# Low words of the experts' weights on one engine, matmuls over ones at the start, and later loads for one attention block, in a fused attention and mixture-of-experts kernel

## The chip, the cores and the metric

The kernel runs on one core of a Trainium2 chip. The metric is the device time of one execution in microseconds (us), as the median of several runs. TensorE (PE) does the matmuls, with its weight loads shown apart (PEld); VectorE (DVE), ScalarE (ACT) and GpSimd (POOL) do elementwise work; SyncE's queue (SPq) issues nearly all DMA transfers.

## The reference

Three stages run one after the other on 4 x 576 = 2304 tokens of 512 features.

```python
# attention: 8 heads of 64, causal window of 128, ALiBi bias, softmax
scores = scale * np.matmul(q, k.transpose(0, 1, 3, 2))
scores = np.where(mask, scores + bias[None], -1000000000.0)
attn = np.exp(scores - np.max(scores, axis=-1, keepdims=True))
x = (attn / (np.sum(attn, axis=-1, keepdims=True) + 1e-09)) @ v
...
# dense feed-forward, 512 -> 2048 -> 512
h = x @ w_in
x = (h - np.tanh(h)) @ w_out
...
# 8 experts, top 1 by cosine similarity, 512 -> 1024 -> 512
expert_idx = np.argmax(xn @ en.T / tau, axis=1)
for e in range(E):
    h = np.maximum(x[mask] @ w1[e], 0.0)
    out[mask] = gate_w[mask, None] * (h @ w2[e])
```

## The kernel before, in words

**Number format.** Most large matmuls are split: an operand becomes a high word (a rounded copy) and a low word (the rest), and three products of the words are added up. For each weight tile of an expert (128 x 512) `e_weight` issues a load into one of six staging tiles `est`, a cast on ACT (`hi`, line 1080) and a subtraction (`lo`, line 1084). The planner may put `lo` on DVE or on POOL, and it frees the staging tile.

**Attention.** The tokens are 18 blocks of 128 rows. A block is done in four quarters of two heads: `scores` (matmuls, line 485 in the first four blocks, 491 later), `soft` (adds the bias tile of the head and takes the extremum, line 513, DVE), `exp` (line 527, ACT), a transpose of the probabilities (lines 548 and 552 early, a transposing DMA at 542 later) and the product with the values (562 early, 573 later). `x_out` transposes the finished block into `xT` (lines 664, 671, 672). Blocks 0 to 3 use the keys and queries unsplit. From block 4 on they are split (`qk_half`: a load into the staging tile `stk`, an ACT cast at line 381, a subtraction at line 385), and so are the values (`v_half`: lines 443 to 454). As block 4 also looks back at block 3, `qk_half` and `v_half` run for block 3's keys and values too. There is one staging tile `stk`, and SPq issues in order: a second load into `stk` waits until line 385 has read the first, and everything behind it in the queue waits as well.

**Bias.** `consts` loads a table (`tmp`) and makes one bias tile for each head from it (line 255): heads 0 and 1 on DVE, heads 2 to 7 on POOL.

**Feed-forward.** Two blocks form a group, so there are nine groups. A `step` makes two slices of 128 hidden features: matmuls into `h` (line 712), tanh on ACT (717), a subtraction (720), high and low word (725, 729), then matmuls into `acc` (736). Eight steps finish a group. All 32 weight tiles of `w_in` and `w_out` stay in SBUF; each is loaded packed (line 335) and unpacked by lines 339, 342, 347 and 351 on ACT and DVE, in the first 80 us.

**Routing and experts.** `route` takes a group's result, finds each token's expert (line 826, the small operations of `chain` at 847 to 852, matmuls at 862 to 865) and scatters the rows. The experts (lines 1186 to 1246) follow; their weights are loaded and split while the last group of the feed-forward still runs, and then one expert ahead.

**Order.** Every operation is a task with a due time and a cost for each engine that may do it. `Plan.order` simulates the engines: it takes the task that can start earliest, then the one with the lowest due time, and picks the engine that would finish it first. The result is a fixed order of instructions for each engine; each engine runs its list in order. The due unit is one step of the feed-forward. Tasks with `port=True` are not started on DVE, in the simulation, while POOL works.

Of the kernel before, what the change touches and what calls it, by code (L numbers as in the profile page):

```python
# [13 lines left out]
BF16 = mybir.dt.bfloat16  # L14
# [3 lines left out]
AF = mybir.ActivationFunctionType  # L18
ALU = mybir.AluOpType
# [20 lines left out]
NF = 4  # L40
# [7 lines left out]
WLEAD2 = 6  # L48
N0 = 1
NPX = 16  # L50
NALT = 8
NOWN = 8
NXO = 2
# [2 lines left out]
QK = 2  # L56
# [122 lines left out]
class Builder:  # L179
# [61 lines left out]
    def zero(self, P):  # L241
        for n, t in enumerate(self.wz):
            P.add({"DVE": 0.6}, lambda e, t=t: self.nc.vector.memset(t, 0), -30, w=[("wz", n)])

    def consts(self, P):
        nc, i = self.nc, self.i
        at = {}

        def tmp(e):
            at[0] = self.at.tile([128, 512], F32, tag="xr", name="tmp", bufs=1)  # L250
            nc.sync.dma_start(out=at[0][:, 0:384], in_=i["c_bias"])

        P.add({"SP": 0.55}, tmp, -20, w=[("xr", m) for m in range(4)])
        for h in range(H):
            P.add({"DVE": 0.3} if h < 2 else {"POOL": 0.88}, lambda e, h=h: self.eng(e).tensor_scalar(
                out=self.bias[:, h, :], in0=at[0][:, 0:256], scalar1=2.0 ** -(h + 1), scalar2=None, op0=ALU.mult),
                -20 + h, r=[("xr", 0)], w=[("bias", h)])
        P.add({"POOL": 0.5}, lambda e: nc.gpsimd.tensor_copy(out=self.tri, in_=at[0][:, 256:384]), -11,
              r=[("xr", 0)], w=["tri"])
# [197 lines left out]
    def quarter(self, P, a, due):  # L457

        nc = self.nc
        b, qd = divmod(a, 4)  # L460
        hf, qq = divmod(qd, 2)
        s, n = b % 2, (2 * b + hf) % 2
        one = b in NOPRE
        W = 128 if one else 256
        v = {"sc": [None, None], "mx": [None, None]}
        pb = a % 2 if a < NPX else 0
        early = b < NF
# [3 lines left out]
        own = 1 if a < NOWN and a % 2 else None  # L471
        bank = "acc" if a < NALT and a % 2 else "sc"

# [140 lines left out]
        for jj in range(2):  # L614
            if early:
                P.add({"PE": 0.3 if one else 0.42}, lambda e, jj=jj: scores(jj), due,
                      r=["at", ("qf", b)] + [("kf", x) for x in ([b] if one else [b, b - 1])], w=[(bank, jj)])
            else:
                P.add({"PE": 0.13 if one else 0.24}, lambda e, jj=jj: scores(jj), due,
                      r=["at"] + ks + [("kl", x, hf) for x in kv] + q, w=[(bank, jj)])  # L620
        for jj in range(2):
            P.add({"DVE": ttr}, lambda e, jj=jj: soft(jj), due, r=["at", ("bias", qd * 2 + jj)],
                  w=[(bank, jj), ("mx", jj, a % 2)])
        for jj in range(2):
            P.add({"ACT": 0.49 if one else 0.64}, lambda e, jj=jj: exp(jj), due,
                  r=["at", (bank, jj), ("mx", jj, a % 2)], w=[("p32", pb, jj), ("sm", sk, qq, jj)])
        sm = [("sm", sk, x, y) for x in range(2) for y in range(2)]
        half = [("xr", 2 * hf), ("xr", 2 * hf + 1)]
        if early:
# [3 lines left out]
                  r=["at", ("tp", a)] + ([("h", own)] if own is not None else []), w=[("pt", a % 2)],  # L633
                  free="misc" if own is None else None)
            P.add({"PE": 0.45 if one else 0.9}, pv_f, due,
                  r=["at", ("pt", a % 2)] + [("vf", x) for x in ([b] if one else [b - 1, b])], w=[("o", qq)] if qq else ["o", ("o", 0), ("o", 1)])
            if qq:
# [4 lines left out]
              w=[("ph", a % 2)], port=True)  # L642
        P.add({"POOL": 0.84, "DVE": 0.46} if one else {"POOL": 1.19, "DVE": 0.71}, s_lo, due,
              r=["at", ("p32", pb, 0), ("p32", pb, 1), ("ph", a % 2)], w=[("ph", a % 2, 1)], port=True)
        P.add({"SP": 0.7 if one else 1.2}, tr, due, late=LATE, r=["at", ("ph", a % 2), ("ph", a % 2, 1)], w=[("pt", a % 2)])
        P.add({"PE": 0.28 if one else 0.56}, pv, due,
              r=["at", ("pt", a % 2)] + [("vt", x, hf, m) for x in kv for m in range(3)], w=["o"])
# [412 lines left out]
    def e_weight(self, P, e, kind, f, due):  # L1060

        nc, i = self.nc, self.i
        ff = f + FE // 128 * (e % 2)
        n = self.nld % NST
        self.nld += 1
        key, st = (kind, ff), ("est", n)
        v = {}
        w1, w2 = [i[w].rearrange("e k f -> (e k) f") for w in ("w1", "w2")]

        def load(_):  # L1070
            t = v["x"] = self.ex.tile([128, 512], F32, tag=f"est{n}", name="est")
            if kind == "i":
                half, k = divmod(f, KD)
                nc.sync.dma_start(out=t, in_=w1[bass.ds(self.at_row[e][0] + k * 128, 128), half * 512:(half + 1) * 512])
            else:
                nc.sync.dma_start(out=t, in_=w2[bass.ds(self.at_row[e][1] + f * 128, 128), :])

        def hi(_):
            t = self.w[key] = self.wp.tile([128, 2, 512], F32R, tag=f"w{kind}{ff}", name=f"e{kind}{ff}")
            nc.scalar.copy(out=t[:, 0, :], in_=v["x"])  # L1080

        def lo(eng):
            t = self.w[key]
            self.eng(eng).tensor_tensor(out=t[:, 1, :], in0=v["x"], in1=t[:, 0, :].bitcast(F32), op=ALU.subtract)

        P.add({"SP": 0.73}, load, due - 4, r=["at", ("place", e)], w=[st], lag=LAG)
        P.add({"ACT": 0.65}, hi, due, r=[st], w=[(key, 0), (key, 1)])
        P.add({"DVE": 0.72, "POOL": 1.32}, lo, due, r=[st, (key, 0)], w=[(key, 1)], port=True)

    def e_rows(self, P, v, t, due):  # L1090

# [249 lines left out]
    def build(self):  # L1341
        tc, nc = self.tc, self.nc
        for n in ("kf", "qf", "vf", "sums", "oh4", "qst", "xr", "acc", "w"):
            setattr(self, n, {})
        self.setup()
        dp = self.pool("dr", bufs=1, space=DRAM, tilewait=False)
        self.bucket = dp.tile([ROWS, ROW], F32, name="bucket")
        self.pa = dp.tile([2 * N0, 128, DM], F32, name="pa")
        self.nw = 0
        self.sent, self.puts = [], []  # L1350
        P = Plan()
        P.add({"POOL": 2.7}, lambda e: self.small(), 0, w=["small", "cum"])
        self.zero(P)
        self.consts(P)
        self.small_loads(P, -19)
        all_f = list(range(FP))
        fa, fb = all_f[:FA], all_f[FA:]
        visits = ([(g, fa) for g in range(N0)] + [(N0, all_f)] + [(g, fb) for g in range(N0)]
                  + [(g, all_f) for g in range(N0 + 1, NG)])

        def weights(fps, due, rate):
            for x, fp in enumerate(fps):
                for kind in "io":
                    for f in (2 * fp, 2 * fp + 1):
                        self.weight(P, kind, f, due + x * rate + 1.2 * (kind == "o"))

        weights(fa, -WLEAD, WRATE)
        p, xi, seen = 0, 0, set()
        for g, fps in visits:
            sl = [xi % XR, (xi + 1) % XR]  # L1370
            xi += 2
            rate = RATE if g <= N0 else 1.0
            for n in range(2):
                b = 2 * g + n
                d0 = p - 8 * rate - (LEADM if g > N0 else LEAD) + 4 * n * rate
                if g not in seen:
                    for hf in range(2):
                        due = d0 + 2 * hf * rate
                        self.qk_half(P, b, hf, due - QK)
                        if b < NF and hf == 0:  # L1380
                            self.qk_early(P, b, due - QK - 2)
                            self.v_full(P, b, due)
                        if b >= NF - 1:
                            self.v_half(P, b, hf, due)
                        for qq in range(2):
                            self.quarter(P, 4 * b + 2 * hf + qq, due + qq * rate)
                if g not in seen:
                    self.x_out(P, b, sl[n], d0 + 4 * rate)
                    if b == 0:
                        self.emb(P, 0)  # L1390
            if g == N0:
                weights(fb, p + len(fa) - WLEAD2, WRATE2)
            for fp in fps:
                self.step(P, p, g, fp, sl, fp == fps[0], fp == fps[-1])
                for e in range(E):
                    if p == PAD + e // PADN:
                        self.pad(P, e, p)
                p += 1
            if g < N0 and g not in seen:
                self.spill(P, p - 1, g, sl)  # L1400
            else:
                if g == NG - 1:
                    self.moe2(P, p, lambda: self.route(P, g, sl, p))
                else:
                    self.route(P, g, sl, p + 1)
                if g == NG - 3:
                    self.choose(P, p + 2)
                    self.space(P, p + 2)
            seen.add(g)
        with tc.manual_schedule():  # L1410
            for fn, e in P.order({"misc": 1}):
                fn(e)
        self.overflow()
        while self.open:
            k = list(self.open)[-1]
            self.close(k)
# [190 lines left out]
```

## Time and profile before

| | us |
|---|---|
| median of 3 runs (lowest to highest) | 781.98 (780.95 to 782.5) |
| profiled execution: device time | 785.27 |
| profiled execution: span of the trace | 783.4 |
| TensorE busy / its weight loads busy | 760.1 / 678.7 |
| DVE / ACT / POOL busy | 549.5 / 427.9 / 382.6 |

The span goes from the first to the last instruction of one execution, and the device time has 1.9 us more around it. Matmuls are pipelined and their ends are modelled, so a busy share near 100% on TensorE doesn't mean that it works at its peak. The granted clock is a column of the view of stretches: 1.00 stands for 2.4 GHz and 0.50 for 1.2 GHz.

### The profile page before, as it was taken

What the parts mean: (1) busy time and instruction counts of PE and PEld (TensorE: products, weight loads), DVE (VectorE), ACT (ScalarE), POOL (GpSimd) and SP (SyncE); (2) the same over time, 40 slices, a digit from 0 to 9 for tenths busy, and PEclk for the clock granted to TensorE, in tenths of its full rate; (3) what the DMA queues carried; (4) which work ended last, traced back from release to release, by engine and by line L of the source; (5) the groups of instructions that cost most, each with busy time, mean ns of one, the idle gap of its engine ahead of it and who ended that gap; (6) DMA issues with size and microseconds to landing.
All of it is one profiled execution on the core that took longest, in us unless ns stands there. A gap on an engine that the chain in (4) does not pass through costs nothing.

```text
span 783.4 us, 15248 instructions
## 1 busy us (share of the span) xinstructions
PE 760.1 (97%) x5189; PEld 678.7 (87%) x5189; DVE 549.5 (70%) x1454; ACT 427.9 (55%) x969; POOL 382.6 (49%) x378
## 2 busy tenths in 40 slices
PE   6998999999999999999999999989999999999996
PEld 4877899889998999989899998979879898888895
DVE  4888887888777688778777776887626678675420
ACT  4878776655565465555645643645235565555321
POOL 3226023674666165364744732687216577655411
PEclk9999999999999999999999999999999999999998
DMA  7996169966365353554454243764257879897100
GB/s 269 385 372 195 44 200 296 247 155 113 108 131 139 69 116 104 119 117 133 95 123 121 62 81 88 184 201 148 76 160 208 230 218 261 216 237 218 44 29 30
DMA packets 152454, 124.25 MB, mean 159 GB/s; under 512 B 115301, under 2 KB 119397, under 8 KB 152112
## 3 DMA queue, kind: packets, MB, share of 16 engines
q1 hardware_dynamic: 149344, 111.39, 53.5%
q0 software_dynamic: 3024, 11.82, 4.1%
q8 instruction: 42, 0.69, 0.4%
q14 instruction: 44, 0.36, 0.2%
HBM read 84.29 MB, written 22.06 MB: 136 GB/s over the span
## 4 chain that ended last, share of the span: by engine, by line
PE 87%; DVE 4%; issue 4%; ACT 2%; POOL 2%; DMA 1%; SPq 0%; POOLq 0%
PE h L712 25%; PE acc L736 23%; PE he L1186 12%; PE y L1221 10%; PE o L573 3%; PE sc L491 3%; PE y L1217 3%; PE of L562 2%; PE sc L485 1%; PE misc L548 1%; PE misc L664 1%; PE ht L1306 1%; DMA tmp<-in_c_bias 1%; PE misc L821 1%; DVE xA L1146 0%
## 5 line engine op out<-in xcount | busy, mean ns | idle before, releaser
L712 PE MATMUL h<-xT,wi 128*128 128x256 f32 x1728 | 227.8, 286 | 0.8 <-DVE xT L672 0.5
L712 PEld LDWEIGHTS h<-xT,wi 128*128 128x128 f32 x1728 | 219.7, 193 | 6.8 <-DVE xT L672 0.7
L736 PE MATMUL acc<-wo,gh 128*128 128x512 f32 x576 | 183.4, 400 | 0.4 <-DVE wo L351 0.4
L736 PEld LDWEIGHTS acc<-wo,gh 128*128 128x128 f32 x576 | 101.0, 190 | 16.6 <-issue 1.0
L736 PE MATMUL acc<-wo,gl 128*128 128x512 f32 x288 | 113.0, 392 | 0.0
L717 ACT ACTIVATE t<-h 128x512 f32<-128x512 f32 x72 | 43.0, 597 | 105.7 <-PE h L712 100.2
L1221 PE MATMUL y<-eo,ge 128*128 128x512 f32 x336 | 88.0, 398 | 0.2 <-ACT yo L1229 0.2
L527 ACT ACTIVATE p<-sc,mx 128x256 f32<-128x256 f32 (+1 forms) x128 | 59.0, 462 | 39.4 <-DVE mx L513 27.4
L1221 PEld LDWEIGHTS y<-eo,ge 128*128 128x128 f32 x336 | 60.1, 188 | 10.5 <-ACT yo L1229 0.4
L729 DVE TENSOR_TENSOR gl<-t,gh 128x512 fp32r<-128x512 f32 x72 | 64.4, 895 | 6.7 <-ACT gh L725 6.4
L537 POOL TENSOR_TENSOR ph<-p,ph 128x512 f16<-128x512 f32 (+1 forms) x37 | 43.9, 1187 | 51.1 <-ACT ph L532 40.5
L736 PEld LDWEIGHTS acc<-wo,gl 128*128 128x128 f32 x288 | 54.3, 189 | 12.2
L385 POOL TENSOR_TENSOR khl<-stk,khl 64x512 fp32r<-64x512 f32 x24 | 31.8, 1325 | 67.3 <-ACT khl L381 61.3
L720 DVE TENSOR_TENSOR t<-h,t 128x512 f32<-128x512 f32 x72 | 49.5, 687 | 18.5 <-ACT t L717 18.2
L1208 DVE SCALAR_TENSOR_TENSOR ge<-he,ge 128x256 fp32r<-128x256 f32 x104 | 28.8, 315 | 46.7 <-ACT ge L1202 46.3
L513 DVE CUSTOM_DVE_ANT_0 sc<-sc,bias 128x256 f32<-128x256 f32 (+1 forms) x136 | 49.6, 374 | 15.5 <-PE sc L491 9.5
L1246 POOL DMA_INDIRECT out<-yo,ix x23 | 25.0, 1089 | 69.9 <-ACT yo L1242 63.0
L1202 ACT ACTIVATE ge<-he 128x288 fp32r<-128x288 f32 (+2 forms) x56 | 23.2, 414 | 61.2 <-PE he L1186 42.5
L1186 PEld LDWEIGHTS he<-xA,ei 128*128 128x128 f32 x384 | 54.1, 189 | 2.6
L1186 PE MATMUL he<-xA,ei 128*128 128x288 f32 (+2 forms) x384 | 56.0, 296 | 0.0
L1186 PEld LDWEIGHTS he<-xT,ei 128*128 128x128 f32 x384 | 53.5, 188 | 2.2
L1186 PE MATMUL he<-xT,ei 128*128 128x288 f32 (+2 forms) x384 | 55.0, 295 | 0.0
(224 smaller groups left out, 1444.3 us busy)
## 6 DMA issues: line engine op xcount, KB each, us to landing
est<-in_w SPq DMA_DIRECT2D x128, 256.0 KB, 3.6
bucket<-in_c_pad SPq DMA_DIRECT2D x8, 1155.0 KB, 9.7
rawi<-in_w_in SPq DMA_DIRECT2D x16, 511.8 KB, 7.3
rawo<-in_w_out SPq DMA_DIRECT2D x16, 511.8 KB, 8.9
stk<-in_k SPq DMA_DIRECT2D x30, 256.0 KB, 2.8
stq<-in_q SPq DMA_DIRECT2D x28, 256.0 KB, 3.0
vst<-in_v SPq DMA_DIRECT2D x30, 128.0 KB, 2.8
xe<-bucket SPq DMA_DIRECT2D x3, 384.0 KB, 3.4
```

The lines of the kernel that those rows point to most:

```text
L385: self.eng(e).tensor_tensor(out=k, in0=r4("k")[64:128], in1=k.bitcast(F32), op=ALU.subtract)
L513: nc.vector.tensor_tensor_reduce(out=x, in0=x, in1=self.bias[:, h, c0:c1], scale=-0.125, scalar=mx[:, 1:2] if m else 3.0e38, op0=ALU.add, ...
L527: nc.scalar.activation(out=v["p32"][:, jj * W:(jj + 1) * W], in_=x, func=AF.Exp, scale=-1.0, bias=v["mx"][jj][:, 0:1], accum_out=self.sums ...
L537: self.eng(e).tensor_tensor(out=ph[:, 2 * W:4 * W], in0=v["p32"][:, 0:2 * W], in1=ph[:, 0:2 * W], op=ALU.subtract)
L712: nc.tensor.matmul(h3(v["h"], f2), lhsT=w[:, a, k, :], rhs=xT[c][:, :, k, :], start=(k == 0 and n == 0), stop=(k == KD - 1 and n == 2))
L717: nc.scalar.activation(out=v["t"], in_=v["h"].rearrange("p a b -> p (a b)"), func=AF.Tanh)
L720: nc.vector.tensor_tensor(out=v["t"], in0=v["h"].rearrange("p a b -> p (a b)"), in1=v["t"], op=ALU.subtract)
L729: self.eng(e).tensor_tensor(out=v["gl"], in0=v["t"], in1=v["gh"].bitcast(F32), op=ALU.subtract)
L736: nc.tensor.matmul(self.acc[g, t], lhsT=v[a][:, c0:c0 + 128], rhs=self.w["o", fs[f2]][:, c, :], start=(first and f2 == 0 and n == 0), stop ...
L1186: nc.tensor.matmul(h[:, 0:N], lhsT=w[:, a, c0:c0 + 128], rhs=xT()[b][:, k, 0:N], start=(k == 0 and n == 0), stop=(k == KD - 1 and n == 2))
L1208: nc.vector.scalar_tensor_tensor(out=g[:, o:o + c1 - c0], in0=hk[f][:, c0:c1], scalar=0.0, in1=g[:, c0:c1].bitcast(F32), op0=ALU.max, op1= ...
L1221: nc.tensor.matmul(y[t], lhsT=gt(f, a)[:, (t - ts[0]) * 128:(t - ts[0] + 1) * 128], rhs=self.w["o", f0 + f][:, b, :], start=(f == 0 and n ...
```

## The change

There are three edits. (1) The low words of the experts' weights are no longer offered to POOL. (2) A bf16 tile `fill` of ones is set by DVE, and 21 matmuls of 128 x 512 over it go to the PSUM bank `h0`, whose result nobody reads: 7 before everything else, 8 behind the scores of quarter 0, and 2 behind the scores of each of quarters 1, 2 and 3. The bias tiles of heads 2 to 7 may now go to DVE, ACT or POOL. (3) For block 3 the loads, casts and subtractions of the keys and of the values are due three steps later.

```diff
+BIAS = [{"DVE": 0.3}, {"DVE": 0.3}] + [{"DVE": 0.3, "ACT": 0.47, "POOL": 0.88}] * 6
+WARM = [7, 8, 2, 2, 2]
...
+    def warm(self, P, n, due, r=()):
+        nc = self.nc
+        def run(e):
+            y = self.misc("h0")
+            for _ in range(n):
+                nc.tensor.matmul(y, lhsT=self.fill[:, 0:128], rhs=self.fill, start=True, stop=True)
+        def begin(e):
+            self.fill = self.m1.tile([128, 512], BF16, tag="gh0", name="fill", bufs=1)
+            nc.vector.memset(self.fill, 1.0)
+        if not r:
+            P.add({"DVE": 0.3}, begin, -40, w=[("gh", 0)])
+        P.add({"PE": 0.22 * n}, run, due, r=[("gh", 0), *r], w=[("h", 0)])
...
+        def slope(e, h):
+            out, src = self.bias[:, h, :], at[0][:, 0:256]
+            if e == "ACT":
+                nc.scalar.activation(out=out, in_=src, func=AF.Copy, scale=2.0 ** -(h + 1))
+            else:
+                self.eng(e).tensor_scalar(out=out, in0=src, scalar1=2.0 ** -(h + 1), scalar2=None, op0=ALU.mult)
         for h in range(H):
-            P.add({"DVE": 0.3} if h < 2 else {"POOL": 0.88}, lambda e, h=h: self.eng(e).tensor_scalar(
-                out=self.bias[:, h, :], in0=at[0][:, 0:256], scalar1=2.0 ** -(h + 1), scalar2=None, op0=ALU.mult),
+            P.add(BIAS[h], lambda e, h=h: slope(e, h),
                 -20 + h, r=[("xr", 0)], w=[("bias", h)])
...
+        if a + 1 < len(WARM) and WARM[a + 1]:
+            self.warm(P, WARM[a + 1], -30, [(bank, 0), (bank, 1)])
...
-        P.add({"DVE": 0.72, "POOL": 1.32}, lo, due, r=[st, (key, 0)], w=[(key, 1)], port=True)
+        P.add({"DVE": 0.72}, lo, due, r=[st, (key, 0)], w=[(key, 1)], port=True)
...
+        self.warm(P, WARM[0], -40)
...
-                        self.qk_half(P, b, hf, due - QK)
+                        late = 3 if b == NF - 1 else 0
+                        self.qk_half(P, b, hf, due - QK + late)
...
-                            self.v_half(P, b, hf, due)
+                            self.v_half(P, b, hf, due + late)
```

## Rows read from the trace of the kernel before

**Rows 1.** The page's part 4: the chain that ended last, by engine.

```profile
PE 87%; DVE 4%; issue 4%; ACT 2%; POOL 2%; DMA 1%; SPq 0%; POOLq 0%
```

**Rows 2.** Stretches: length, busy us (count) by engine, clock, DMA share, GB/s.

```profile
16.00:20.00 4.00, 4.00 (x22) 2.83 (x20) 2.80 (x15) 2.83 (x11) 1.27 (x1) 1.00 0.27 95
40.00:54.00 14.00, 14.00 (x89) 11.09 (x86) 10.55 (x30) 11.10 (x26) 2.26 (x5) 1.00 1.03 406
...
68.00:74.00 6.00, 5.24 (x28) 4.97 (x29) 5.09 (x12) 5.55 (x15) 3.45 (x3) 0.72 0.19 56
500.00:522.00 22.00, 18.82 (x138) 16.87 (x136) 20.80 (x23) 13.82 (x26) 20.66 (x15) 1.00 0.62 186
522.00:528.00 6.00, 5.60 (x28) 5.01 (x29) 4.53 (x13) 2.31 (x5) 3.46 (x4) 0.72 0.54 178
640.00:700.00 60.00, 60.00 (x348) 53.46 (x347) 44.66 (x86) 34.46 (x67) 38.02 (x32) 1.00 0.84 230
```

**Rows 3.** The chain in order of time: start, us, what.

```profile
8.46 0.62 PE misc L548 x2
...
17.66 0.49 PE scx L485
...
33.29 1.63 PE h L712 x12
...
94.33 2.75 PE acc L736 x12
```

**Rows 4.** Timeline of PE, 0 to 20 us: start, us, instruction, [idle before <- releaser].

```profile
7.67 0.79 PE L485 MATMUL sc<-kf,qf 64*128 64x128 f32 x2 [2.29 <-ACT p L527]
...
15.55 0.63 PE L485 MATMUL sc<-kf,qf 64*128 64x256 f32 x1
...
17.99 0.38 PE L485 MATMUL sc<-kf,qf 64*128 64x256 f32 x1
```

**Rows 5.** Waits of the SP queue to 34 us: us, times, longest.

```profile
SPq L375 <- POOL khl L385: 6.9, 1, 6.9
```

**Rows 6.** Timeline of all engines, 0 to 16 us: the bias tiles.

```profile
6.16 0.69 DVE L255 TENSOR_SCALAR bias<-tmp 128x256 bf16<-128x256 f32 x2 [4.25 <-DMA tmp<-in_c_bias]
6.22 5.48 POOL L255 TENSOR_SCALAR bias<-tmp 128x256 bf16<-128x256 f32 x6 [4.55 <-DMA tmp<-in_c_bias]
```

**Rows 7.** Waits of PE, whole span: us, times, longest.

```profile
PE misc L862 <- DVE oh L852: 3.6, 1, 3.6
PE sc L491 <- ACT p L527: 3.1, 3, 2.7
```

**Rows 8.** Groups of DVE, 498 to 523 us: busy us, mean ns, idle before.

```profile
L1084 DVE TENSOR_TENSOR ei<-est,ei 128x512 fp32r<-128x512 f32 x2 | 3.4, 1710 | 0.0
...
L830 DVE TENSOR_TENSOR lg<-lg,rs 128x16 f32<-128x16 f32 x1 | 1.3, 1312 | 0.0
...
L847 DVE TENSOR_REDUCE rs<-lg 128x2 f32<-128x16 f32 x1 | 0.2, 155 | 0.0
```

**Rows 9.** Groups of POOL, 498 to 523 us.

```profile
L1084 POOL TENSOR_TENSOR ei<-est,ei 128x512 fp32r<-128x512 f32 x7 | 10.9, 1559 | 1.3 <-ACT ei L1080 1.3
L1084 POOL TENSOR_TENSOR eo<-est,eo 128x512 fp32r<-128x512 f32 x6 | 9.5, 1589 | 0.0
```

**Rows 10.** Line 1084, whole span: count, shortest/median/longest ns, first and last start.

```profile
L1084 DVE TENSOR_TENSOR ei<-est,ei x36: 669/689/1815, 499.9 to 730.1; 128x512 fp32r<-128x512 f32 x36
L1084 POOL TENSOR_TENSOR eo<-est,eo x32: 1263/1356/1759, 500.9 to 727.7; 128x512 fp32r<-128x512 f32 x32
...
L1084 POOL TENSOR_TENSOR ei<-est,ei x28: 1268/1304/1810, 502.6 to 726.0; 128x512 fp32r<-128x512 f32 x28
```

**Rows 11.** Groups of DVE, 640 to 700 us.

```profile
L1084 DVE TENSOR_TENSOR ei<-est,ei 128x512 fp32r<-128x512 f32 x12 | 11.6, 966 | 3.6 <-ACT ei L1080 3.6
```

**Rows 12.** Groups of POOL, 640 to 700 us.

```profile
L1084 POOL TENSOR_TENSOR eo<-est,eo 128x512 fp32r<-128x512 f32 x9 | 12.3, 1365 | 2.4 <-ACT eo L1080 2.3
L1084 POOL TENSOR_TENSOR ei<-est,ei 128x512 fp32r<-128x512 f32 x7 | 9.6, 1367 | 2.9 <-ACT ei L1080 2.9
```

## Prediction

> **What bounds the kernel now.** I read the chain that ended last first: TensorE stands for 87% of it [rows 1]. So a microsecond is won only where TensorE waits or runs slowly, and time saved on another engine counts only through that. Then I cut the span into stretches to find those places [rows 2]. From 640 to 700 us TensorE is busy for all 60.00 us at granted clock 1.00, and nearly all of the middle looks like this. Three places differ.
>
> First the start. The chain names TensorE without a break from 8.46 us to 17.66 us, and at nearly every step from there past the first feed-forward matmuls at 33.29 us [rows 3]. Yet the matmul over 64x256 takes 0.63 us at 15.55 us and 0.38 us at 17.99 us [rows 4]. Same form, same data types: the array ran at its lower level (1.2 GHz) until about 17.7 us and at 2.4 GHz after. The column of the granted clock does not show it: it says 1.00 for 16 to 20 us [rows 2]. The reader is to take the clock of the start from durations of one form, not from that column. Before 7.67 us TensorE had stood idle for 2.29 us [rows 4].
>
> Second, 65 to 74 us: TensorE waits up to 2.7 us on one quarter's softmax [rows 7], and the mean granted clock from 68 to 74 us is 0.72 [rows 2].
>
> Third, the hand-over to the experts: TensorE waits 3.6 us for `oh`, the end of the routing chain on DVE [rows 7], and then has a mean clock of 0.72 from 522 to 528 us [rows 2]. Just before, from 500 to 522 us, DVE is busy for 20.80 of 22 us and POOL for 20.66 [rows 2].
>
> DMA is a fourth, hidden one: its share is 1.03 with 406 GB/s from 40 to 54 us, but 0.27 with 95 GB/s from 16 to 20 us [rows 2]. There the SP queue stood 6.9 us behind the second load into `stk` [rows 5].
>
> **Part 1: matmuls over ones, and the bias tiles.** The matmuls fill TensorE before the first data and in the 2.29 us gap. What they can give back: the 9.2 us from 8.46 to 17.66 us, at the ratio of one form before and after the rise, 0.38/0.63 = 0.60, so 9.2 x 0.40 = 3.7 us. (At a pure ratio of two it would be 4.6, the upper bound; nothing is the lower.) That the clock would hold through this patchy work I take from the trace: the same mix of scores, transposes and small products, with no feed-forward matmul in it until 33.29 us [rows 3], kept its full rate from 17.7 us on.
>
> Their cost: 128x512 matmuls in a dense run at full clock start 2.75/12 = 0.23 us apart [rows 3], so at half clock some 0.46. The trace has no bf16 ones; I take these. Seven end near 4.6 us if they start near 1.3; softmax can't begin before the bias table at 6.16 us [rows 6], which covers them. The eight behind quarter 0 need 1.8 us (fast) to 3.7 us (slow), against a hole that ended at 7.67 us; quarter 1's scores stand behind them. I take 0.5 us late, bounds 0 to 1.5. The six of the later quarters fall into waits for softmax. The memset of `fill` is under the 6 us in which DVE has little else.
>
> The bias tiles would cap the gain: six of them in a row on POOL take 5.48 us, to 11.70 [rows 6]. On three engines they need about two each; DVE takes 0.35 us for one [rows 6], so all are there by about 7.5 us. This is no gain of its own; it lets the faster TensorE have its inputs, at the price of one or two tiles ahead of the first softmax (0.3 to 0.7 us, inside the 0.5 above). Net for part 1: 3.7 - 0.5 = 3.2 us.
>
> **Part 2: block 3's loads later.** Four loads move, two of keys and two of values, and with them two casts and two subtractions for the keys and four of each for the values. Their 768 KB (by the tile sizes) are 1.9 us at 406 GB/s; they leave one stretch in which DMA is full for another, so the transfers end no later, and the first steps' weights come that much sooner. With the second load into `stk` gone from its place, SPq goes on to the packed weights, and the hole of 16 to 20 us is filled: 4 x (406 - 95)/406 = 3.1 us of transfer come back. Weights then arrive about as much earlier as TensorE does, which is why part 1 need not die at 40 to 54 us, where DMA is full. What is late next is block 3's own split, by its due times now around 36 to 54 us; block 4's scores, steps later, need it. There POOL has 2.26 us of work in 14 and DVE 10.55 [rows 2], so room exists. But a POOL instruction can hold up a DVE one by about 1.0 us (1710 ns against the usual 689) [rows 8, 10]; six such, at worst 6 us on DVE with 3.45 us of idle time. I charge 0.7, bounds 0 to 2.5. The stall at 65 to 74 us is bounded by 3.1 us of waits [rows 7] and 6 x 0.28 = 1.7 us of clock; earlier weights could shorten it and more work on POOL could lengthen it. I take 0. Parts 1 and 2 together: 3.2 - 0.7 = 2.5 us, bounds -4.0 (0 - 1.5 - 2.5) to 4.6, or 9.4 if the stall goes too.
>
> **Part 3: low words on DVE.** The 60 instructions on POOL (about 1.3 us each) become 60 on DVE of 0.69 us [rows 10]. From 498 to 523 us there are 13 of them [rows 9], so DVE gets 13 x 0.69 = 9.0 us more. What it loses: an L830 over 128x16 takes 1312 ns while POOL works, when the reduction L847 next to it, as small, takes 155 [rows 8]. Of DVE's 23 instructions from 500 to 522 us I count 14 held up like that, at some 0.85 us each: 12 us. So DVE's 20.8 us become 20.8 - 12 + 9.0 = 17.8, about 3 us sooner, and the chain from L830 on shrinks most: three more of its small operations (L848, L849, L852) were held up alike, one after the other. The wait of 3.6 us and the 6 x 0.28 = 1.7 us of lost clock behind it make 5.3 us; bounds 0 to 5.3. I take 4.5, near the upper end, since the routing chain is due before most of the new instructions.
>
> The Trainium skill, SBUF: State Buffer, section "Who interferes with whom", says that GpSimd and VectorE share one pair of ports as an exclusive lock, that two-input VectorE operations on SBUF wait out a GpSimd one that reads SBUF, and that a reduction never does. L830 and L847 agree with it to the letter. By that rule all 12 us come back; a plain reading of the busy sums, without it, would add 9.0 us to an engine with 1.2 us free and make the hand-over some 8 us worse.
>
> In the experts' stage: from 640 to 700 us DVE is busy 44.66 us [rows 2], 16 instructions move [rows 12], 16 x 0.69 = 11.0 us; its own 23 low words there (12 at 966 ns, 11 alike) give back 23 x 0.28 = 6.4 us [rows 11]. So 49 of 60: TensorE stays the bound, cost nothing. That cover is checked in the last rival.
>
> **The sum.** 2.5 + 4.5 = 7.0 us. Against the profiled execution: span 783.4 to 776.4, device time 785.27 to 778.3. The median of the runs shown, 781.98, lies 3.3 us below that execution, so I forecast 781.98 - 7.0 = 775.0.
>
> **Rivals.**
> *The clock falls back.* After the 21 matmuls TensorE returns to short matmuls with gaps, and the lower level comes back until about 17 us; then part 1 gives nothing and the ones cost up to 1 us. For it: this mix ran from 7.67 to 17.7 us without raising the clock. Against it: the same mix held it afterwards. Time: 781.98 - 4.5 + 0.5 = 778. The Trainium skill, TensorE: Matmul & The Clock Gate, Part 4, says that transposes do not count as activity in the way matmuls do, which would favour this rival; the rows speak against it: after 17.7 us the full rate held with the transposes of lines 548 and 664 among the rest.
> *The hand-over stays.* DVE is so full that `oh` is no earlier, part 3 gives 0: 781.98 - 2.5 = 779.5. For it: only 3 us of computed slack.
> *The change doesn't do what it says.* The lead of the start is eaten by 82 us, where DVE unpacks the last weights, and the hand-over stays: 781 to 783.5, the same.
> *Slower: DVE queues in the experts.* Each expert's activation low word (line 1208) sits in DVE's order, and each of the 60 moved instructions can stand 0.69 us in front of it. If a share reaches TensorE, the gain of 7.0 us is gone from 10 of 60 on (7.0/0.69); at 20 of 60 the time is 775.0 + 13.8 = 789. For it: were DVE's low words to stay at 966 ns, 44.66 + 16 x 0.97 = 60.2 of 60 us would be full. Against: most of what makes them 966 is the work that leaves POOL.
>
> **Chances.** Forecast, 772 to 778: 0.50. Better, the stall at 65 to 74 us also shrinks (its 4.8 us), 767.5 to 772: 0.13. Clock falls back, 778: 0.12. Hand-over stays, 779.5: 0.10. Nothing moves: 0.07. Slower: 0.08. About 0.2% (1.6 us) is what can be told from no change. Faster 0.84, same 0.08, slower 0.08. The range of 767.5 to 780.5 leaves out the last two cases; it takes in the best of the bounds (781.98 - 9.4 - 5.3 = 767.3) almost whole.
>
> **What would show it.** Right: the 64x256 matmul takes 0.38 us well before 10 us; the first `h` matmul comes 3 us or more before 33.29 us; no 6.9 us wait of `stk`; the wait of L862 is under 1 us, clock 1.00 from 500 to 530 us; L830 takes 0.16 us; DVE near 49 of 60 us beside a TensorE that never waits. Wrong: small matmuls back at their slow durations before 17 us; a new wait on `wi`, `wo` or `xT` before 82 us as long as the lead; L862 still waiting; gaps of TensorE behind line 1208.

## The result and the profile after

The changed kernel takes 773.85 us (median of 11 runs, 772.88 to 781.28) where the kernel before takes 781.57 beside it (11 runs, 780.06 to 784.95): a ratio of 0.991, 95% interval 0.989 to 0.993, or 7.7 us. Forecast were 775.0 us, range 767.5 to 780.5. Two of the eleven runs of the changed kernel took 779.90 and 781.28 us, at a mean granted clock of 0.992 and 0.989 where the other nine have 0.995 to 0.999: what the change gains is not there in every execution, and no trace of those two was kept. The profiled executions lie further apart, 785.27 and 773.49 us (spans 783.4 and 771.7), because the one of before was 3.7 us above its median. A second profile of the kernel before (e9 below) has 782.12 us and a span of 780.3, and is the fairer base.

Line numbers of the changed kernel are higher: 485 is now 510, 491 is 516, 712 is 739, 736 is 763, 830 is 857, 862 is 889, 1084 is 1111. The ones are line 254.

The page's part 4 (the chain that ended last) of the changed kernel, beside [rows 1]. TensorE's share went up from 87% to 89%, and POOL's 2% are gone:

```profile
PE 89%; DMA 4%; issue 3%; DVE 2%; ACT 1%; POOL 0%; SPq 0%; POOLq 0%; ACTq 0%; DVEq 0%
```

Its stretches, with the columns of [rows 2] (length, busy us and count of PE, PEld, DVE, ACT, POOL, granted clock, DMA share, GB/s):

```profile
16.00:20.00 4.00, 4.00 (x30) 3.09 (x29) 3.71 (x14) 3.83 (x14) 0.00 (x0) 1.00 1.03 408
...
68.00:74.00 6.00, 6.00 (x41) 5.51 (x40) 5.44 (x15) 4.68 (x11) 1.23 (x1) 1.00 0.16 40
500.00:522.00 22.00, 22.00 (x166) 20.02 (x165) 18.46 (x47) 11.93 (x23) 2.44 (x4) 1.00 0.80 233
522.00:528.00 6.00, 6.00 (x39) 5.47 (x38) 4.74 (x9) 4.63 (x9) 0.00 (x0) 1.00 0.85 260
640.00:700.00 60.00, 59.61 (x346) 52.87 (x345) 42.86 (x102) 35.17 (x69) 22.32 (x20) 1.00 0.86 237
```

The three weak stretches of [rows 2] are mended: DMA moves 408 GB/s from 16 to 20 us (95 before), 68 to 74 us has a clock of 1.00 and a busy TensorE (0.72 before), and so has the hand-over from 500 to 528 us. In the experts' stage DVE carries all low words and is busy 42.86 of 60 us, less than the 44.66 before.

TensorE's timeline at the start (start, us, instruction, idle before it), which answers to [rows 4]:

```profile
1.43 3.17 PE L254 MATMUL misc<-fill 128*128 128x512 bf16 x7 [1.43 <-DVE fill L258]
4.53 0.80 PE L510 MATMUL sc<-kf,qf 64*128 64x128 f32 x4
5.26 2.55 PE L254 MATMUL misc<-fill 128*128 128x512 bf16 x8
7.74 0.49 PE L510 MATMUL scx<-kf,qf 64*128 64x128 f32 x4
...
15.48 0.38 PE L510 MATMUL sc<-kf,qf 64*128 64x256 f32 x1
...
30.45 1.69 PE L739 MATMUL h<-xT,wi 128*128 128x256 f32 x12 [0.32 <-DVE xT L699]
```

Seven ones take 3.17 us, eight 2.55: the array comes to its full rate (2.4 GHz) among the eight. Four scores that take 0.80 us at 4.53 take 0.49 at 7.74, and the 64x256 form takes 0.38 us at 15.48 (0.63 at 15.55 before). The first feed-forward matmul starts 2.8 us sooner.

The chain of the changed kernel to that matmul (start, us, what):

```profile
5.69 5.47 DMA qf<-in_q
...
11.17 9.03 DMA rawo<-in_w_out
...
20.22 8.87 DMA ec<-in_emb
...
29.11 0.68 DVE sq L309
...
29.79 0.61 DVE xT L699
...
30.45 1.57 PE h L739 x11
```

TensorE held the chain here before [rows 3]; now it is transfers. DVE takes its work in order, and `sq`, which waits until 29.1 us for the small load of the experts' embeddings behind the weights, stands in front of the `xT` that the matmul needs. But a chain names what came last, not what there is to win: TensorE stood idle for 0.32 us only before that matmul (the row at 30.45 above), since it had attention work until then.

At the hand-over, groups of DVE from 498 to 523 us (busy us, mean ns, idle before), beside [rows 8]. The small two-input operation that took 1312 ns takes 176, and the wait for `oh` of 3.6 us [rows 7] is no longer in the list of TensorE's waits:

```profile
L857 DVE TENSOR_TENSOR lg<-lg,rs 128x16 f32<-128x16 f32 x1 | 0.2, 176 | 0.0
L875 DVE TENSOR_TENSOR eq<-lg,rs 128x16 f32<-128x16 f32 x1 | 0.2, 176 | 0.0
```

**Where the 8.6 us between the spans of 780.3 and 771.7 come from**, by the start of the same matmul in both timelines (all 864 `acc` matmuls are recorded in both): the 813th `acc`, ahead of the hand-over, and the 843rd, behind it, first in e9 (with its first `h`), then in the changed kernel.

```profile
33.82 1.69 PE L739 MATMUL h<-xT,wi 128*128 128x256 f32 x12
...
517.03 0.39 PE L763 MATMUL acc<-wo,gl 128*128 128x512 f32 x1
...
534.99 0.39 PE L763 MATMUL acc<-wo,gl 128*128 128x512 f32 x1
```

```profile
510.30 0.39 PE L763 MATMUL acc<-wo,gl 128*128 128x512 f32 x1
...
526.00 0.39 PE L763 MATMUL acc<-wo,gl 128*128 128x512 f32 x1
```

The first `h` starts at 33.82 us in e9 and at 30.45, so the lead is 3.4 us there, 6.7 ahead of the hand-over and 9.0 behind it; 0.4 are lost again by the end. At the 300th `acc` (226.36 and 219.76 us) it is 6.6 already. So about 3.4 us are the start, 3.3 come between it and 226 us, where the largest wait of e9 is the stall at 65 to 74 us, and 2.3 are the hand-over.

### The profile page after: what moved, and what is told of

It is laid out like the page before. It is cut to its first block, busy times and chain, and to the rows that moved or that the text cites. A ratio compares the mean times of both kernels' runs of the same rounds, so it can differ in the third digit from the quotient of the medians.

```text
span 771.7 us, 15244 instructions
## 1 busy us (share of the span) xinstructions
PE 758.2 (98%) x5210; PEld 673.8 (87%) x5210; DVE 550.8 (71%) x1502; ACT 429.5 (56%) x973; POOL 309.3 (40%) x327
## 4 chain that ended last, share of the span: by engine, by line
PE 89%; DMA 4%; issue 3%; DVE 2%; ACT 1%; POOL 0%; SPq 0%; POOLq 0%; ACTq 0%; DVEq 0%
PE h L739 27%; PE acc L763 26%; PE he L1213 12%; PE y L1248 10%; PE o L598 4%; PE sc L516 4%; PE y L1244 3%; DMA rawo<-in_w_out 1%; DMA ec<-in_emb 1%; PE misc L691 1%; PE ht L1333 1%; DMA qf<-in_q 1%; PE misc L848 1%; DMA est<-in_w 1%; PE of L587 1%
## 5 line engine op out<-in xcount | busy, mean ns | idle before, releaser
L756 DVE TENSOR_TENSOR gl<-t,gh 128x512 fp32r<-128x512 f32 x72 | 59.6, 828 | 5.9 <-ACT gh L752 5.6
L538 DVE CUSTOM_DVE_ANT_0 sc<-sc,bias 128x256 f32<-128x256 f32 (+1 forms) x136 | 49.5, 373 | 17.7 <-PE sc L516 14.1
L410 POOL TENSOR_TENSOR khl<-stk,khl 64x512 fp32r<-64x512 f32 x25 | 33.7, 1349 | 50.6 <-ACT khl L406 43.3
```

Source lines behind the costliest of these rows:

```text
L410: self.eng(e).tensor_tensor(out=k, in0=r4("k")[64:128], in1=k.bitcast(F32), op=ALU.subtract)
L538: nc.vector.tensor_tensor_reduce(out=x, in0=x, in1=self.bias[:, h, c0:c1], scale=-0.125, scalar=mx[:, 1:2] if m else 3.0e38, op0=ALU.add, ...
L756: self.eng(e).tensor_tensor(out=v["gl"], in0=v["t"], in1=v["gh"].bitcast(F32), op=ALU.subtract)
```

## The experiments

Each edit is on the changed kernel, or on the kernel before where it says "alone". Ratios are to the kernel before, run beside it (medians 781.22 us for e1 to e4, 781.83 for the others). The planner orders the work anew for every edit, so a run differs from its neighbours in the order of the work as well as in the part that is named.

| run | kernel | median us | ratio, 95% interval |
|---|---|---|---|
| e1_ones | ones alone | 777.67 | 0.9942, 0.9920 to 0.9963 |
| e2_low | low words alone | 778.76 | 0.9971, 0.9957 to 0.9985 |
| e3_late | late loads alone | 782.75 | 1.0019, 0.9999 to 1.0039 |
| e4_bias | bias tiles alone | 785.66 | 1.0051, 1.0031 to 1.0071 |
| e5_no_low | all but the low words | 775.08 | 0.9923, 0.9903 to 0.9942 |
| e6_no_ones | all but the ones | 785.14 | 1.0037, 1.0018 to 1.0056 |
| e7_no_late | all but the late loads | 776.72 | 0.9935, 0.9916 to 0.9953 |
| e8_no_bias | all but the bias tiles | 774.78 | 0.9914, 0.9888 to 0.9940 |
| e9_same | before, once more | 782.12 | one run |
| e10_seven | only the first seven ones | 783.91 | 1.0024, 1.0006 to 1.0043 |
| e11_emb | embeddings ten steps later | 780.75 | 0.9993, 0.9981 to 1.0005 |
| e12_emb_no_bias | e11 and e8 together | 780.73 | 0.9989, 0.9977 to 1.0001 |

### The ones alone, and all but the ones

e1 is the kernel before with this alone; e6 is the changed kernel without it:

```diff
+WARM = [7, 8, 2, 2, 2]
...
+        self.warm(P, WARM[0], -40)
...
+        if a + 1 < len(WARM) and WARM[a + 1]:
+            self.warm(P, WARM[a + 1], -30, [(bank, 0), (bank, 1)])
```

> Only the matmuls over ones are added to the kernel before (bias tiles, loads and low words stay as they were). My theory: the 64x256 scores matmul takes 0.38 us from about 9 us on, but heads 2 to 7 still wait for POOL's bias tiles (to 11.7 us) and the SP queue still stands behind the second load into stk, so the first matmul into h comes 1 to 2 us sooner than 33.2 us and the median is 1 to 2 us below the kernel before (about 780). Rival, the clock is all there is to the start: 3 us or more at the first matmul into h and 778.5. Rival, the ones only delay: no gain, 782 or more. The wait for oh before the experts stays in all three (3 to 4 us).

> The changed kernel without the 21 matmuls over ones (bias tiles on three engines, late loads and low words stay). If the parts add up as measured alone: +1.5 (loads) + 4.4 (bias) - 2.5 (low words) = 784 to 785. If bias tiles and late loads harm only through chance of the order: about 779, that is the kernel before less what the low words gave. In both, the small matmuls run at their slow durations to about 17 us and the first matmul into h comes 2 us or more after that of the changed kernel.

The ones carry the change: 0.58% alone, and without them the other three parts together are slower than before (785.14 us, as the sum of the parts alone had it, 784 to 785). How much of this is the clock itself and how much the new order is not separated. That e6 starts late for want of the clock, and not of data, its PE timeline shows: there is no hole in DMA (408 GB/s from 16 to 20 us, as in the changed kernel), and yet

```profile
18.95 0.63 PE L510 MATMUL sc<-kf,qf 64*128 64x256 f32 x1
...
21.70 0.38 PE L510 MATMUL sc<-kf,qf 64*128 64x256 f32 x1
```

Two things in e1 contradict the prediction's reasoning. Its first `h` starts at 28.43 us, 2 us sooner than in the changed kernel, with POOL making six bias tiles as before. Half of the 2 us is there by quarter 0: in e1's execution the full rate came sooner, and the eight ones end 1.0 us earlier.

```profile
4.46 0.49 PE L510 MATMUL sc<-kf,qf 64*128 64x128 f32 x4
4.88 1.90 PE L254 MATMUL misc<-fill 128*128 128x512 bf16 x8
```

And the hole in DMA is gone without any load moved: the wait for the second load into `stk` is 2.0 us (6.9 before [rows 5]), and DMA moves 399 GB/s from 16 to 20 us. Before, the cast of the first `stk` on ACT stood behind a copy that had waited 3.24 us for TensorE's transposes; in e1 the cast stands ahead of the first such copy. So a slow TensorE and the place in ACT's order made that wait together. ACT's rows, of before and then of e1:

```profile
15.07 0.37 ACT L552 COPY ptf<-misc 128x256 f32<-128x256 f32 x1 [3.24 <-PE misc L548]
...
16.14 0.62 ACT L381 CAST khl<-stk 128x512 fp32r<-128x512 f32 x1
```

```profile
11.01 0.62 ACT L406 CAST khl<-stk 128x512 fp32r<-128x512 f32 x1 [0.81 <-DMA stk<-in_k]
```

PE's stretches in e1 (length, busy us and count, clock, DMA share, GB/s) show what the ones cured and what they brought:

```profile
64.00:74.00 10.00, 9.93 (x73) 1.00 0.25 44
150.00:154.00 4.00, 1.75 (x11) 1.00 1.06 157
154.00:160.00 6.00, 5.63 (x50) 0.72 0.51 123
```

The stall at 65 to 74 us [rows 2, 7] is gone with the ones alone. The other runs agree as far as they go: with the full set of ones and the old embeddings TensorE is busy for 8.8 to 9.9 of these 10 us at a clock of 1.00 (e1, e5, e7, e8 and the changed kernel); without it, for 6.8 to 8.2 (before, e2, e3, e4, e6, e9, e10), though the clock there is 1.00 in e4, e6 and e10 and 0.83 in the rest. A new one stands at 154 us, in PE's waits of e1:

```profile
PE misc L848 <- DVE xT L699: 2.6, 1, 2.6
...
PE misc L889 <- DVE oh L879: 2.1, 1, 2.1
```

It costs 2.6 us and a clock of 0.72 for the 6 us behind it, and the wait for `oh` is left as well. e1 gains 0.58% only.

### Late loads alone, and all but the late loads

```diff
-                        late = 3 if b == NF - 1 else 0
+                        late = 0
```

This is e7's edit; e3 is the kernel before with the later due times alone.

> Only block 3's loads, casts and subtractions are due three steps later. My theory: the SP queue no longer waits 6.9 us and DMA stays near 400 GB/s from 16 to 20 us, but TensorE is the bound there at the lower clock, so by itself it gives 0 to 1 us (about 781); earlier weights may shorten the stall at 65 to 74 us, worth up to 4.8 us on top. Rival, the DMA hole was what set the start: 2.5 us or more at the first matmul into h.

> The changed kernel with block 3's loads at their old due times. My theory, parts that need each other: TensorE, fast from 6 us on, now finds the queue standing behind the second load into stk and the weights late; the time is 2 us or more above the changed kernel (776 or more), with DMA below 300 GB/s somewhere between 14 and 20 us. Rival, the parts add up (late loads alone cost 1.5 us): 772.5, faster than the changed kernel.

Alone they bring nothing (1.5 us slower, the interval reaches to no change), though the hole is filled as expected (409 GB/s from 16 to 20 us) and the first `h` starts at 32.22 us. In the combination they seem worth some 2 us: 0.9935 without against 0.9910 with them, but the intervals overlap, so this is not shown. e7's time is that of its theory, its mechanism is not: DMA moves 401 GB/s from 14 to 20 us. PE's waits of e7 name the place, the stall of e1 over again (the clock from 154 to 160 us is 0.72 too), where the changed kernel has no such wait:

```profile
PE misc L848 <- DVE xT L699: 2.6, 1, 2.6
```

So what the late loads go with is the lack of a stall at 154 us, which the kernel before doesn't have either, and not the hole at 16 to 20 us: e1 and e7 have the ones without the late loads and stall there, while e5, e8 and the changed kernel have both and do not (in e6, with the late loads and without the ones, the same wait is 1.3 us and the clock stays at 1.00). How the loads' place leads to that wait stays open.

### Low words alone, and all but the low words

```diff
-        P.add({"DVE": 0.72, "POOL": 1.32}, lo, due, r=[st, (key, 0)], w=[(key, 1)], port=True)
+        P.add({"DVE": 0.72}, lo, due, r=[st, (key, 0)], w=[(key, 1)], port=True)
```

This is e2's edit, on the kernel before; e5 takes it out of the changed kernel.

> Only the low words of the experts' weights go to VectorE alone; the start is that of the kernel before. My theory: the wait of L862 for oh falls from 3.6 us to under 1 us, the granted clock is 1.00 from 500 to 530 us, L830 takes 0.16 us, and the median falls by 4 to 5.5 us, to about 777. Rival, the hand-over was cured by the earlier start: the wait stays above 2 us and the gain is below 1.5 us. Rival, VectorE's queue delays the experts: TensorE waits behind line 1208, and the time is not below the kernel before.

> The changed kernel with the low words offered to POOL again (ones, bias tiles and late loads stay). If the parts add up as they measured alone, it is 2 to 3 us above the changed kernel, near 776.5. My theory: TensorE waits for oh again (2 us or more) and L830's successor of 128x16 takes about 1.2 us again; everything to 490 us as in the changed kernel. Rival, the earlier start cures the hand-over: no wait above 1 us and 774.

Alone they give 0.29%, 2.3 us, where 4 to 5.5 were expected; in the combination 0.13%, 1.0 us, which these intervals do not tell from nothing. The mechanism is as forecast: in e2 no wait for `oh` is left, the clock is 1.00 from 500 to 528 us and L857 takes 175 ns; and in e5, with POOL at work again, DVE's groups from 488 to 523 us read

```profile
L857 DVE TENSOR_TENSOR lg<-lg,rs 128x16 f32<-128x16 f32 x1 | 1.1, 1056 | 0.0
...
L874 DVE TENSOR_REDUCE rs<-lg 128x2 f32<-128x16 f32 x1 | 0.2, 155 | 0.0
```

The Trainium skill, SBUF — State Buffer, "Who interferes with whom", says that a VectorE operation with two SBUF inputs contends with a GpSimd one that reads SBUF, and that a reduction does not; the trace agrees (1056 and 155 ns). But e5 waits only 0.9 us for `oh`, not 2 or more, with a clock of 1.00 behind, which is the wait that its rival named: in that order of the work little is left to win.

### Bias tiles alone, and all but the bias tiles

```diff
-BIAS = [{"DVE": 0.3}, {"DVE": 0.3}] + [{"DVE": 0.3, "ACT": 0.47, "POOL": 0.88}] * 6
+BIAS = [{"DVE": 0.3}, {"DVE": 0.3}] + [{"POOL": 0.88}] * 6
```

This is e8's edit; e4 is the kernel before with the spread alone.

> Only the bias tiles of heads 2 to 7 may go to VectorE, ScalarE or GpSimd. My theory: all tiles are there by about 7.5 us instead of 11.7, but TensorE at the lower clock is the bound from 8.5 us on, so the gain is 0 to 0.7 us (about 781). Rival, the tiles on GpSimd set the start: the first matmul into h comes 1.5 us or more sooner than 33.2 us.

> The changed kernel with heads 2 to 7's bias tiles on POOL alone again. My theory, parts that need each other: the fast TensorE waits for POOL's tiles until 11.7 us, and the time is 1 us or more above the changed kernel (775 or more). Rival, the parts add up (bias tiles alone cost 4.4 us): about 769.5, clearly faster than the changed kernel.

With the spread all tiles are there by 7.2 us, against 11.70 [rows 6]; timeline of the changed kernel, ACT, DVE and POOL:

```profile
5.69 1.03 ACT L276 ACTIVATE bias<-tmp 128x256 bf16<-128x256 f32 x3 [3.70 <-DMA tmp<-in_c_bias]
...
5.69 1.19 DVE L278 TENSOR_SCALAR bias<-tmp 128x256 bf16<-128x256 f32 x4 [3.24 <-DMA tmp<-in_c_bias]
...
6.21 0.99 POOL L278 TENSOR_SCALAR bias<-tmp 128x256 bf16<-128x256 f32 x1
```

Beside the ones it has no worth that can be told (0.9914 without, 0.9910 with it), so both theories of e8 fell, and alone it costs 0.5%. Why it costs that much alone stays open: every instruction behind it is placed anew, and e4's trace shows waits scattered between 30 and 110 us (1.9 us on `gl`, 1.8 on a softmax), not one cause.

### The kernel before, once more

> The same instructions as the kernel before, run once more with a profile, to see which of the profiled execution's losses belong to the kernel and which to that one execution (785.27 us, 3.7 above the median of 781.57). Theory: the stall at 65 to 74 us with its fall of the clock and the wait of 3.6 us for oh come back, and the time is about 781.5 only because the falls of the granted clock (0.72 from 68 to 74 us and from 522 to 528 us) are shorter by 2 to 4 us in sum. Rival: waits and clock are as in the first execution, and the 3.7 us are spread over the span.

PE's waits, and its stretches (length, busy us and count, clock, DMA share, GB/s):

```profile
PE sc L516 <- ACT p L552: 2.7, 1, 2.7
...
PE misc L889 <- DVE oh L879: 2.1, 1, 2.1
```

```profile
64.00:74.00 10.00, 6.81 (x43) 0.83 0.37 119
500.00:522.00 22.00, 19.91 (x148) 1.00 0.66 193
522.00:528.00 6.00, 6.00 (x41) 1.00 0.57 184
```

The stall at 65 to 74 us is back with its loss of clock (6.8 us of work in 10, clock 0.83): it belongs to the kernel. The hand-over came out otherwise than either theory had it: the wait is 2.1 us in place of 3.6, and the clock does not fall. The 5.3 us from which the prediction took its 4.5 were those of one execution; this one lost 2.1 there.

### Only the first seven ones

```diff
-WARM = [7, 8, 2, 2, 2]
+WARM = [7, 0, 0, 0, 0]
```

> The changed kernel with the first seven matmuls over ones alone, without the fourteen behind the quarters. Theory that the clock rises only once a dense stretch has lasted longer than the seven: the 64x256 matmul stays at 0.63 us until 15 us or later, and the time is that of the run without ones, about 785 (ratio 1.003). Rival, that the seven are enough or nearly so: 0.38 us well before 10 us and a time within 1.5 us of the changed kernel, 773.9 to 775.4 (ratio 0.990 to 0.992).

The time is that of the first theory, the course that of neither. PE's timeline:

```profile
5.11 0.41 PE L510 MATMUL scx<-kf,qf 64*128 64x128 f32 x4
7.17 0.49 PE L510 MATMUL sc<-kf,qf 64*128 64x128 f32 x2 [1.65 <-ACT p L552]
...
8.17 0.27 PE L510 MATMUL sc<-kf,qf 64*128 64x128 f32 x1
...
10.12 0.79 PE L510 MATMUL scx<-kf,qf 64*128 64x128 f32 x2
...
19.27 0.63 PE L510 MATMUL sc<-kf,qf 64*128 64x256 f32 x1
...
22.27 0.38 PE L510 MATMUL sc<-kf,qf 64*128 64x256 f32 x1
```

In this execution the seven do raise the clock (four scores take 0.41 us at 5.11, and took 0.78 at 4.52). Then TensorE waits 1.65 us for the first softmax, works on at the full rate until about 8.5 us and falls back, until about 22 us. The stretches show the same fall:

```profile
8.00:16.00 8.00, 7.91 (x26) 0.53 1.02 399
16.00:20.00 4.00, 4.00 (x15) 0.50 1.03 408
```

So the seven are lost here without the fourteen later ones, 8 in the first gap and 6 between the quarters. Its mean clock over the span is 0.989; of the other eleven five have 0.986 to 0.990, and six have 0.995 to 0.999 with times of 777.75 to 785.40 us. As the column does not show a start at the lower level, the seven may not have raised the clock at all in those six; no trace of them was kept. Whether the fourteen would do alone was not tried, and whether the gap or the short matmuls behind it let the clock fall, this run does not separate.

### Embeddings later, without and with the old bias tiles

```diff
-                        self.emb(P, 0)
+                        self.emb(P, 10)
```

> The changed kernel with the load of the expert embeddings and the work on it due ten steps later, so that on DVE the xT that the first feed-forward matmul needs stands ahead of the instruction that waits for that load. Theory that this wait now sets the start: the first h matmul begins near 28.5 us in place of 30.45, and the time falls by 1 to 2 us, to 772 to 773 (ratio 0.988 to 0.990). Rival: the weights or the attention set the start by 42 us anyway, h begins sooner and waits later, and the time is that of the changed kernel (ratio 0.990 to 0.992).

> The same later embeddings, with bias tiles 2 to 7 on POOL alone as before the change: a version with less of the change in it. Theory that the spread of the bias tiles is worth nothing once the ones are there: within 0.2% of the run with later embeddings alone. Rival, that POOL's tiles, ready at some 11 us, hold the quicker start once nothing else does: 2 us or more slower than that run, first h matmul later by as much.

Both theories of e11 fell: the first `h` starts at 30.30 us, 0.15 sooner, and the kernel is 7 us slower than the changed one. TensorE has no idle time ahead of that `h` in e11, and had 0.32 us in the changed kernel, so there were 0.3 us to win there and not 2. The wait moved along with the load: on DVE's timeline, and then on PE's,

```profile
54.51 0.68 DVE L309 CUSTOM_DVE_ANT_0 sq<-ec 8x512 f32<-8x512 f32 x1 [0.93 <-DMA ec<-in_emb]
```

```profile
59.73 0.38 PE L320 MATMUL misc<-con,ec 8*128 8x8 f32 x4 [1.53 <-DVE ec L315]
```

Four tiny transposes that wait for `ec` hold TensorE for 1.5 us, and its stretches show a clock at its lower level behind them, and 4.9 us of idle time much later (48.88 of 50 us are busy there in the changed kernel):

```profile
62.00:68.00 6.00, 5.13 (x15) 3.95 (x15) 5.90 (x12) 4.56 (x12) 4.41 (x8) 0.54 0.20 69
150.00:200.00 50.00, 45.12 (x368) 40.00 (x367) 40.21 (x119) 25.67 (x66) 30.36 (x31) 1.00 0.56 131
```

The later part is block attention in an order that the edit rearranged. How much of the 7 us is due to the embeddings themselves and how much to that order stays open. e12 agrees with e11 to 0.1%, as its theory had it, so the bias tiles are worth nothing here either. No run has a shorter median than the changed kernel.

## Why the prediction was right, step by step

The forecast of 7.0 us met 7.7 measured, but two of its terms were off in opposite directions, so that the sum came out is luck to that extent.

**The start, 3.2 us: right in size.** The first `h` comes 2.8 us sooner than in the first profile, a little under the 3 that were to show it, and 3.4 than in the second. The seven ones ended at 4.60 (forecast 4.6), the eight took 2.55 us (1.8 to 3.7).

**"I take 0" for the stall at 65 to 74 us: this step failed.** I left it out for want of a reason; the wait on that softmax went, and the fall of the clock with it, and with the ones alone both are gone as well (e1). That the slow start made it is borne out by the runs with and without the ones, but as the order differs too, not every step to it is shown. With it parts 1 and 2 give 6.7 us in place of 2.5; the stall's going had a chance of 0.13.

**The hand-over, 4.5 us: mechanism right, size wrong.** L830's operation fell to 176 ns, the wait went, the clock held. But the 5.3 us were read from one execution; the second had 2.1 us to lose, and with the other edits in place e5 loses 0.9. Measured are 2.3 us between the traces against e9, 2.3 by the ratio of e2 and about 1 in the combination. The rival "the hand-over stays" fell, as `oh` is in time, but this term came out midway between the rival's 0 and the forecast.

**"The bias tiles would cap the gain": failed.** e8 shows the same speed without the spread, and e1 an earlier first `h`. The tiles themselves came as forecast (7.2 us, forecast 7.5).

**The late loads, a charge of 0.7: wrong sign in the combination.** The hole at 16 to 20 us goes without them (e1). Their worth of some 2 us, if it is one, goes with the stall at 154 us, which in its full length only the runs with the ones and without the late loads have.

**"The clock would hold through this patchy work": the inference failed, the forecast held.** I took it from the same mix holding its rate after 17.7 us, and gave the later ones a price but no part in holding the clock. e10 has that mix at the full rate at 8 us and loses it. Half of the rival "the clock falls back" is so right: it falls in e10, where the later ones do not fill the gaps, and holds where they do. The rule on transposes that stood beside that rival (the Trainium skill, TensorE: Matmul & The Clock Gate, Part 4) is not decided by it: in e10 the mix with transposes fell, in the changed kernel it held with ones among it.

**The experts' stage, nothing:** right. DVE has 42.86 of 60 us, not 49, because its low words take 742 to 808 ns, not 966, beside a POOL that is busy for 22.32 us in place of 38.02; the slower rival found nothing to act on.

The parts do not add up: alone they make -0.58, -0.29, +0.19 and +0.51%, in sum -0.17%, and together -0.90%. Without the ones they do add up (+0.41 in sum, +0.37 in e6): what goes beyond the sum needs the ones.

## What to carry to other kernels

Matmuls that compute nothing paid here while they kept TensorE without a gap until its real work was dense; stopped too soon they were lost, so price what they hold as well as what they cost. A stall some way behind a slow stretch may be its echo: look whether it hangs on work that the slow stretch delayed before you bound it at nothing. Before you move what a chain names, read how long the bounding engine stood idle there. Take a wait's price from two executions of the same program, and test an edit among the others as well as alone, since here, with TensorE busy for 98% of the span, one edit took a wait away at 65 us and another came up at 154.

## What the hardware showed that was not expected

The same instructions lost 3.6 us and then 6 us at a clock of 0.72 at the hand-over in one execution [rows 2, 7], and 2.1 us at 1.00 in another (e9). Waits of 2.6 and 2.7 us elsewhere were each followed by 6 us at 0.72 (e1, e7, e9). In e4 a wait of 2.1 us at the same place was followed by 0.72 as well, and in e7 one of 2.0 us in the experts' stage (0.72 from 668 to 674 us), so the length of the wait alone does not tell.

The same seven ones and four scores also met different clocks: in e1 the scores behind the seven take 0.49 us, in the changed kernel 0.80, and the full rate comes only among the eight.

The column of the granted clock reads 1.00 in the kernel before and in e6 at 16 to 20 us, when the 64x256 matmul takes 0.63 us; in e10, with the same durations, it reads 0.50. In these traces it showed a fall, not a start at the lower level.
